# Attention by heads through HBM and a feed-forward stage after it, rewritten as units of 384 tokens with both interleaved on chip

## The chip, the cores and the metric

The kernel runs on one core of one Trainium2 chip. The metric is the device time of one execution in microseconds. Five engines work from queues of their own and wait for one another by semaphores: PE (TensorE, matrix products into PSUM, with weight loads shown as PEld), DVE (VectorE), ACT (ScalarE), POOL (GpSimd) and SP (SyncE, here the queue that issues DMAs).

## What is computed

Attention with a routing mask, then a gated feed-forward over the heads joined together. Batch 4, 8 heads, 768 positions, head size 64, 16 clusters; 3072 tokens of width 512, and 1536 hidden units.

```python
q_assign = argmax(q_n . c_n)            # nearest of 16 centroids, per head
k_assign = argmax(k_n . c_n)
mask = q_assign[:, :, :, None] == k_assign[:, :, None, :]
scores = where(mask, scale * q @ k.T, -1e9)
attn = softmax(scores);  x = attn @ v   # heads side by side: 3072 x 512
xn = x / rms(x) * rms_g
g = xn @ w_gate;  val = xn @ w_val
out = (g * sigmoid(g) * val) @ w_out
```

The norm of q and of k changes no argmax, so neither kernel divides by it.

## The kernel before

There are three stages, one after another. The attention loop (L59 to L138) goes over 4 batches and 8 heads. A head's q, k and v come in as six tiles of 128 positions. PE turns each q and k tile (L93, L97, float32, 64 columns out of 128 positions); ACT makes a bf16 copy and DVE a float32 copy. The cluster scores are float32 products of 16 rows (L108), two for q and two for k; POOL finds the largest of the 16 with an all-reduce over partitions (L113), and DVE makes the one-hot tiles `q_ohT` and `k_ohT` (L114). Then, for each of 6 key tiles and 2 query halves of 384, PE computes the scores (L121, 64 rows) and the mask as a product of one-hots (L123, 16 rows); ACT takes the exponential (L126) and DVE multiplies it with the mask from PSUM into `pT` (L127). The value products (L132) have a column of ones, which gives the softmax sum; DVE divides (L134, L136), and the bf16 result goes to `x_scratch` in HBM.

After the last head the feed-forward weights are loaded and cast (L146 to L161). Then 6 chunks of 512 tokens follow (L169 to L208): `x_sb` is read back, DVE and ACT compute the root mean square, PE transposes (L186), and for each of 12 slices of 128 hidden units four products give `gps` (L194) and four `vps` (L196); ACT computes Silu (L199), DVE the product (L200); 12 products for each 128 tokens give the output (L205), which DVE copies (L207).

The order of instructions within an engine's queue is chosen by the tile scheduler by its own costs; pools of 2 or 3 buffers limit how far the stages overlap. The activation tables change between square root, exponential and Silu (57 loads in the first stage, 44 in the last).

Of the kernel before, what the change touches and what calls it, by code (L numbers as in the profile page):

```python
# [9 lines left out]
F32 = mybir.dt.float32  # L11
F32R = mybir.dt.float32r
BF16 = mybir.dt.bfloat16
AX = mybir.AxisListType.X
ALU = mybir.AluOpType
ACT = mybir.ActivationFunctionType


@with_exitstack
def kernel(  # L20
# [15 lines left out]
    d_model = moe_w_gate.shape[0]  # L36
    d_ff = moe_w_gate.shape[1]
    n_tokens = B * S
    assert H * D == d_model
    P = 128  # L40
    ST = S // P
    scale = 1.0 / (D ** 0.5)
    MM = 384
    NM = S // MM

    x_scratch = nc.dram_tensor("x_scratch", (n_tokens, d_model), BF16, kind="Internal").ap()

    const_pool = ctx.enter_context(tc.tile_pool(name="const", bufs=1))
    ident = const_pool.tile([P, P], BF16)
    make_identity(nc, ident)  # L50
    ident_f32 = const_pool.tile([P, P], F32)
    make_identity(nc, ident_f32)

    with tc.tile_pool(name="attn_sbuf", bufs=2) as sb, \
         tc.tile_pool(name="attn_sbuf1", bufs=2) as sb1, \
         tc.tile_pool(name="attn_psum_a", bufs=2, space=bass.MemoryType.PSUM) as psa, \
         tc.tile_pool(name="attn_psum", bufs=2, space=bass.MemoryType.PSUM) as ps:

        for b in range(B):  # L59
            for h in range(H):  # L60
                q_in = sb.tile([P, ST, D], F32, tag="q_in")
                k_in = sb.tile([P, ST, D], F32, tag="k_in")
                v_in = sb.tile([P, ST, D + 1], F32, tag="v_in")
                nc.sync.dma_start(out=q_in, in_=q[b, h].rearrange("(t p) d -> p t d", p=P))
                nc.sync.dma_start(out=k_in, in_=k[b, h].rearrange("(t p) d -> p t d", p=P))
                nc.sync.dma_start(out=v_in[:, :, :D], in_=v[b, h].rearrange("(t p) d -> p t d", p=P))
                nc.vector.memset(v_in[:, :, D:D + 1], 1.0)
                v_bf = sb.tile([P, ST, D + 1], BF16, tag="v_bf")
                nc.vector.tensor_copy(v_bf, v_in)

                c_in = sb.tile([NC, D], F32, tag="c_in")
                nc.sync.dma_start(out=c_in, in_=centroids[h])
                c_sq = sb.tile([NC, D], F32, tag="c_sq")
                nc.vector.tensor_mul(c_sq, c_in, c_in)
                c_ss = sb.tile([NC, 1], F32, tag="c_ss")
                nc.vector.reduce_sum(c_ss, c_sq, axis=AX)
                c_inv = sb.tile([NC, 1], F32, tag="c_inv")
                nc.vector.reciprocal(c_inv, c_ss)
                nc.scalar.activation(c_inv, c_inv, ACT.Sqrt)
                c_n = sb.tile([NC, D], F32, tag="c_n")  # L80
                nc.vector.tensor_scalar_mul(c_n, c_in, c_inv)
                cnt_ps = psa.tile([D, NC], F32, tag="tmp")
                nc.tensor.transpose(cnt_ps, c_n, ident_f32[:NC, :NC])
                c_nT = sb.tile([D, NC], F32, tag="c_nT")
                nc.vector.tensor_copy(c_nT, cnt_ps)

                qT = sb.tile([D, ST, P], BF16, tag="qT")
                kT = sb.tile([D, ST, P], BF16, tag="kT")
                qT32 = sb.tile([D, S], F32, tag="qT32")
                kT32 = sb.tile([D, S], F32, tag="kT32")  # L90
                for t in range(ST):
                    ttmp = psa.tile([D, P], F32, tag="tmp")
                    nc.tensor.transpose(ttmp, q_in[:, t, :], ident_f32)  # L93
                    nc.scalar.copy(qT[:, t, :], ttmp)  # L94
                    nc.vector.tensor_copy(qT32[:, t * P:(t + 1) * P], ttmp)  # L95
                    ttmp2 = psa.tile([D, P], F32, tag="tmp")
                    nc.tensor.transpose(ttmp2, k_in[:, t, :], ident_f32)  # L97
                    nc.scalar.copy(kT[:, t, :], ttmp2)  # L98
                    nc.vector.tensor_copy(kT32[:, t * P:(t + 1) * P], ttmp2)  # L99

                q_ohT = sb.tile([NC, S], BF16, tag="q_ohT")
                k_ohT = sb.tile([NC, S], BF16, tag="k_ohT")
                qT_flat = qT[:, :, :].rearrange("d t p -> d (t p)")
                for (src_T, ohT) in ((qT32, q_ohT), (kT32, k_ohT)):
                    scT_sb = sb1.tile([NC, S], F32, tag="scT_sb")
                    for m in range(NM):
                        scT_ps = ps.tile([NC, MM], F32, tag="scores")
                        nc.tensor.matmul(scT_ps, lhsT=c_nT,  # L108
                                         rhs=src_T[:, m * MM:(m + 1) * MM],
                                         start=True, stop=True)  # L110
                        nc.scalar.copy(scT_sb[:, m * MM:(m + 1) * MM], scT_ps)  # L111
# [127 lines left out]
```

## Time and profile before

| | |
|---|---|
| median of 3 runs | 1066.64 us (1065.25 to 1066.80) |
| span of the profiled execution | 1065.2 us |
| one head in the steady part of attention | 24.28 us |
| attention, to the last product | about 786 us |
| weights loaded and cast | about 50 us |
| feed-forward | 229.2 us |
| POOL in its all-reduce | 166.1 us, idle before it 598.7 us |
| the chain that ended last, by engine | PE 57%, issue 23%, POOL 7%, DVE 4%, ACT 4%, DMA 4% |

The span runs from the first to the last instruction of one profiled execution; the medians are of runs timed as a whole. In the slices each digit is the busy share of a fortieth of the span in tenths, and PEclk is the clock granted to PE in tenths of full speed, as far as its records go. Busy times of PE are modelled, and overlap: the distance from one start to the next says more than the duration.

### The profile page before, as it was taken

The page shows a single profiled execution, that of the slowest core. Times are in us where ns is not written, and L with a number is a line of the kernel's source. Part 1 is how long each engine was busy: PE and PEld are TensorE (multiplying, and loading weights), DVE is VectorE, ACT ScalarE, POOL GpSimd, SP SyncE. Part 2 cuts the span into 40 slices and gives each one's busy share as a digit, 9 for nine tenths or more (in the row PEclk, how much of TensorE's full clock was granted, in tenths as well). Part 3 has the DMA queues.
Part 4 walks back from the last instruction along what each step waited for, and adds up shares of the span by engine and source line. Part 5 has one row for each costly group of instructions (what it writes and reads, how often), then busy time and mean ns, then how long its engine had stood idle before and what let it go on. Part 6 is the DMA issues. An engine that isn't in the chain of part 4 may idle for free.

```text
span 1065.2 us, 11986 instructions
## 1 busy us (share of the span) xinstructions
PE 908.9 (85%) x3552; PEld 311.0 (29%) x3552; DVE 598.0 (56%) x1665; ACT 508.9 (48%) x1221; POOL 167.2 (16%) x72
## 2 busy tenths in 40 slices
PE   4999999988888999999888898989950599999998
PEld 1222223222222222232222222223210244444443
DVE  3556666566656666666666666655542445534533
ACT  3555555555565544545554455444420456536721
POOL 2112111222211111111222111122200000000000
PEclk9999999995555555555555656555555699999999
DMA  3111111111111111111111111111015310110111
GB/s 75 27 26 27 27 26 27 39 41 29 36 27 35 27 27 27 27 27 34 35 28 35 28 27 27 26 26 21 5 58 210 110 55 11 59 50 30 41 40 40
DMA packets 114098, 41.82 MB, mean 39 GB/s; under 512 B 105328, under 2 KB 108400, under 8 KB 114032
## 3 DMA queue, kind: packets, MB, share of 16 engines
q1 hardware_dynamic: 114032, 41.05, 14.9%
q8 instruction: 28, 0.46, 0.2%
q14 instruction: 38, 0.31, 0.1%
HBM read 31.59 MB, written 9.44 MB: 39 GB/s over the span
## 4 chain that ended last, share of the span: by engine, by line
PE 57%; issue 23%; POOL 7%; DVE 4%; ACT 4%; DMA 4%; POOLq 0%; SPq 0%; DVEq 0%; ACTq 0%
PE scT_ps L108 11%; PE mk_ps L123 9%; PE sc_ps L121 8%; POOL sc_max L113 6%; PE gps L194 6%; PE ops L205 6%; PE vps L196 6%; PE ttmp L97 4%; PE ttmp L93 3%; PE acc L132 3%; DMA wo_tmp<-in_moe_w_out_dram 1%; ACT scT_sb L111 1%; PE tps L186 1%; ACT xnT L187 1%; DMA wtmp<-in_moe_w_val_dram 1%
## 5 line engine op out<-in xcount | busy, mean ns | idle before, releaser
L127 DVE TENSOR_TENSOR pT<-p_e,mk_ps 128x384 bf16<-128x384 bf16 x384 | 209.9, 553 | 157.1 <-PE mk_ps L123 140.3
L113 POOL PARTITION_ALL_REDUCE sc_max<-scT_sb x64 | 166.1, 2602 | 598.7 <-ACT scT_sb L111 597.5
L123 PE MATMUL mk_ps<-q_ohT,k_ohT 16*128 16x384 bf16 x384 | 184.8, 498 | 45.5 <-DVE o_sb L136 41.1
L121 PE MATMUL sc_ps<-qT,kT 64*128 64x384 bf16 x384 | 182.8, 492 | 23.5 <-ACT p_e L126 22.0
L126 ACT ACTIVATE p_e<-sc_ps 128x384 bf16<-128x384 f32 x384 | 168.3, 483 | 18.0 <-DVE pT L127 11.7
L98 ACT CAST kT<-ttmp 64x128 bf16<-64x128 f32 x192 | 49.6, 258 | 175.9 <-PE ttmp L97 174.4
L111 ACT COPY scT_sb<-scT_ps 16x384 f32<-16x384 f32 x128 | 59.6, 466 | 107.9 <-PE scT_ps L108 107.8
L194 PE MATMUL gps<-xnT,wg 128*128 128x512 bf16 x288 | 106.3, 396 | 0.8 <-ACT sg L199 0.2
L196 PE MATMUL vps<-xnT,wv 128*128 128x512 bf16 x288 | 105.9, 394 | 0.0
L132 PE MATMUL acc<-v_bf,pT 128*128 128x65 bf16 x1152 | 93.9, 244 | 7.2 <-DVE o_sb L136 6.6
L123 PEld LDWEIGHTS <-k_ohT 16*128 16x128 bf16 x384 | 37.6, 100 | 212.7 <-issue 138.7
L132 PEld LDWEIGHTS <-pT 128*128 128x128 bf16 x1152 | 77.0, 131 | 57.5 <-DVE qT L95 22.1
L108 PE MATMUL scT_ps<-qT,c_nT 64*16 64x384 f32 x128 | 93.0, 829 | 0.1
L94 ACT CAST qT<-ttmp 64x128 bf16<-64x128 f32 x192 | 49.4, 257 | 86.1 <-PE ttmp L93 85.9
L97 PE MATMUL ttmp<-ident_f,k_in 128*64 128x128 f32 x192 | 79.7, 415 | 9.7 <-DVE kT L99 5.5
L108 PE MATMUL scT_ps<-kT,c_nT 64*16 64x384 f32 x128 | 87.0, 794 | 0.0
L200 DVE TENSOR_TENSOR gvT<-sg,vps 128x512 bf16<-128x512 f32 x72 | 47.7, 685 | 67.8 <-ACT sg L199 67.1
L93 PE MATMUL ttmp<-ident_f,q_in 128*64 128x128 f32 x192 | 79.9, 416 | 1.0 <-DVE qT L95 1.0
L187 ACT COPY xnT<-tps 128x128 bf16<-128x128 bf16 x96 | 21.5, 266 | 105.0 <-DVE wo L161 51.4
L121 PEld LDWEIGHTS <-kT 64*128 64x128 bf16 x384 | 35.9, 101 | 108.1 <-issue 104.8
L186 PE MATMUL tps<-ident,xn 128*128 128x128 bf16 x96 | 19.6, 238 | 55.2 <-ACT xnT L187 53.7
L205 PE MATMUL ops<-wo,gvT 128*128 128x512 bf16 x288 | 66.7, 379 | 0.0
(47 smaller groups left out, 762.1 us busy)
## 6 DMA issues: line engine op xcount, KB each, us to landing
q_in<-in_q_dram SPq DMA_DIRECT2D x32, 192.0 KB, 2.5
k_in<-in_k_dram SPq DMA_DIRECT2D x32, 192.0 KB, 2.5
v_in<-in_v_dram SPq DMA_DIRECT2D x32, 192.0 KB, 2.5
out_dram<-out_sb SPq DMA_DIRECT2D x24, 256.0 KB, 2.0
x_scratch<-o_sb SPq DMA_DIRECT2D x192, 16.0 KB, 1.5
x_sb<-x_scratch SPq DMA_DIRECT2D x24, 128.0 KB, 2.0
wtmp<-in_moe_w_gate_dram SPq DMA_DIRECT2D x1, 3072.0 KB, 10.0
wtmp<-in_moe_w_val_dram SPq DMA_DIRECT2D x1, 3072.0 KB, 10.3
```

The costliest lines, as they stand in the source:

```text
L93: nc.tensor.transpose(ttmp, q_in[:, t, :], ident_f32)
L97: nc.tensor.transpose(ttmp2, k_in[:, t, :], ident_f32)
L108: nc.tensor.matmul(scT_ps, lhsT=c_nT, rhs=src_T[:, m * MM:(m + 1) * MM], start=True, stop=True)
L113: nc.gpsimd.partition_all_reduce(sc_max, scT_sb, NC, bass_isa.ReduceOp.max)
L121: nc.tensor.matmul(sc_ps, lhsT=kT[:, kc, :], rhs=qT_flat[:, m * MM:(m + 1) * MM], start=True, stop=True)
L123: nc.tensor.matmul(mk_ps, lhsT=k_ohT[:, kc * P:(kc + 1) * P], rhs=q_ohT[:, m * MM:(m + 1) * MM], start=True, stop=True)
L126: nc.scalar.activation(p_e, sc_ps, ACT.Exp, scale=scale)
L127: nc.vector.tensor_mul(pT[:, kc, m * MM:(m + 1) * MM], p_e, mk_ps)
L132: nc.tensor.matmul(acc, lhsT=pT[:, kc, qg * P:(qg + 1) * P], rhs=v_bf[:, kc, :], start=(kc == 0), stop=(kc == ST - 1))
L194: nc.tensor.matmul(gps, lhsT=wg[:, dc, fc * P:(fc + 1) * P], rhs=xnT[:, dc, :], start=(dc == 0), stop=(dc == DC - 1))
L196: nc.tensor.matmul(vps, lhsT=wv[:, dc, fc * P:(fc + 1) * P], rhs=xnT[:, dc, :], start=(dc == 0), stop=(dc == DC - 1))
L205: nc.tensor.matmul(ops, lhsT=gvT[:, fc, s * P:(s + 1) * P], rhs=wo[:, fc, :], start=(fc == 0), stop=(fc == FC - 1))
```

## The change

The whole body is rewritten, with an order written out by hand in place of the scheduler's.

The work is cut into units of 384 queries: two units for each batch, eight units in all, and groups of four heads, two for each batch. A *group's preparation* (`group_work`) turns q and k of a head together (`trans`: six float32 transposes a head with 128 columns out, ACT copies them to `qkT`, POOL casts q into `qext` and v into `vbf`, DVE casts k divided by 2048 into `kext`) and computes the cluster scores of four heads as float32 products whose 32 output rows lie in four column strips of the array (`scores_c`). DVE transposes these in blocks of 32, finds the maximum, compares, and transposes back; DMAs put the one-hots under q and k in `qext` and `kext`, as rows 64 to 79, with a row of -1 and +1 below them. So the score product contracts 81 rows: the scaled score, plus 1 where the clusters agree, minus 1. With the exponential's scale of 2048/8 a pair of different clusters gives exp(-256 + score), which is 0, and the mask products and the multiplication by the mask are gone. One exponential covers two key tiles (768 columns in two PSUM banks).

A unit's loop goes over 8 heads with three pairs of key tiles each. Behind each pair stands a part of the list `fill`: the output products of the unit two before, then the feed-forward of the unit before, with the preparation of the group two ahead spread between its pieces. Transposes, clusters, gate, value and output products all use one PSUM pool of three buffers (`ps_g`, tag `gen`). Attention's result stays on chip (`xs`). The root is taken with an integer guess and three Newton steps on DVE; the square sums are taken by ACT. Silu is g/2 (1 + tanh(g/2)), with tanh on ACT and two DVE products, so that the table of the exponential stays; only the last unit uses Silu. The weights are cast by 11 DMAs on POOL's queue, between the first and the second group's preparation.

```diff
+    stage = pool("stage", NSTG)
+    qk32 = pool("qk32", 1)
+    ps_s = pool("ps_s", 2, space=PSUM)
+    ps_a = pool("ps_a", 1, space=PSUM)
+    ps_g = pool("ps_g", 3, space=PSUM)
...
+    def trans(g, h, part):
...
+        for i in range(HT):
+            nc.tensor.transpose(ps[:, i * P:(i + 1) * P], qk[:, t].rearrange("p a d -> p (a d)"), ident_f)
+        nc.scalar.copy(qkT[g][:, h, part * UQ:(part + 1) * UQ], ps)
+        if part:
+            nc.gpsimd.tensor_copy(qext[g % 4][:D, h], qkT[g][:D, h])
+            nc.vector.tensor_scalar_mul(kext[g % 4][:D, h], qkT[g][D:, h], 1.0 / ZS)
+            nc.gpsimd.tensor_copy(vbf[g % 4][:, h, :, :D], vs)
+            load(g * HG + h + NSTG)
...
-                        nc.tensor.matmul(scT_ps, lhsT=c_nT,
-                    nc.gpsimd.partition_all_reduce(sc_max, scT_sb, NC, bass_isa.ReduceOp.max)
+        for h in range(HG):
+            nc.tensor.matmul(ps[32 * h:32 * h + 32], lhsT=cblk[:, h0 + h], rhs=qkT[g][:, h, m * UQ:(m + 1) * UQ],
+        nc.vector.transpose(scT[g][:, m * UQ:(m + 1) * UQ], ps)
+        if m:
+            nc.vector.tensor_reduce(mx, cl, axis=AX, op=ALU.max)
+            nc.vector.tensor_tensor(ohT.rearrange("p (n c) -> p n c", c=NC), cl,
+            nc.vector.transpose(oh, ohT)
+            for h in range(HG):
+                nc.sync.dma_start(out=qext[g % 4][D:D + NC, h], in_=oh[32 * h:32 * h + NC])
...
-                        nc.tensor.matmul(mk_ps, lhsT=k_ohT[:, kc * P:(kc + 1) * P], rhs=q_ohT[:, m * MM:(m + 1) * MM],
-                        nc.vector.tensor_mul(pT[:, kc, m * MM:(m + 1) * MM], p_e, mk_ps)
+            nc.tensor.matmul(ps[:, j, :UQ], lhsT=kext[g % 4][:KR, hh, kc * P:(kc + 1) * P],
+                             rhs=qext[g % 4][:KR, hh, hf * UQ:(hf + 1) * UQ], start=True, stop=True)
+        nc.scalar.activation(pT[u, h][:, 2 * i:2 * i + 2], ps[:, :, :UQ], ACT.Exp, scale=scale * ZS)
...
+    def gv(u, f, val):
...
+        ps = ps_g.tile([P, UQ], F32, tag="gen", name="val" if val else "gate")
+        for c in range(CC):
+            nc.tensor.matmul(ps, lhsT=w[:, c, f * P:(f + 1) * P], rhs=xnT[u][:, c], start=c == 0, stop=c == CC - 1)
...
+                nc.scalar.activation(th, ps, ACT.Tanh, scale=0.5)
+                nc.vector.scalar_tensor_tensor(gu, th, 1.0, ps, op0=ALU.add, op1=ALU.mult)
...
+            nc.vector.scalar_tensor_tensor(gvT[u][:, f], gates[u], 0.5, ps, op0=ALU.mult, op1=ALU.mult)
...
+    for _, f in group_work(0):
+        f()
+    load_weights()
+    for _, f in group_work(1)[:2 * HG]:
+        f()
...
+        for h in range(H):
+            for i in range(3):
+                scores(u, h, i)
+                if i == 0 and (u, h) != (0, 0):
+                    pv(u, h - 1) if h else pv(u - 1, H - 1)
+                    if h == 0:
+                        rms(u - 1)
+                while n < len(fill) and done <= total * (3 * h + i + 1) / gaps:
+                    done += fill[n][0]
+                    fill[n][1]()
+                    n += 1
...
+    pv(NU - 1, H - 1)
+    rms(NU - 1)
+    for _, f in out_work(NU - 2) + ffn_work(NU - 1) + out_work(NU - 1):
```

On PE, in the middle of a head's score loop, before (score, mask and a transpose for the next head by turns):

```order
L121 LDWEIGHTS kT
L121 MATMUL sc_ps<-qT,kT 128x384
L123 LDWEIGHTS k_ohT
L123 MATMUL mk_ps<-q_ohT,k_ohT 128x384
L93 MATMUL ttmp<-ident_f_63,q_in 64x128
L121 LDWEIGHTS kT
```

and in a full unit of the change, from the end of its feed-forward part to the start of the next unit (`val` is a value-branch product, `s` a score, `sc` the clusters of group 4 and `acc` a value product of attention):

```order
L275 LDWEIGHTS wv
L275 MATMUL val<-xnT,wv 128x384
L205 LDWEIGHTS kext_148
L205 MATMUL s<-qext_144,kext_148 128x384
L205 LDWEIGHTS kext_148
L205 MATMUL s<-qext_144,kext_148 128x384
L177 MATMUL sc<-qkT,cblk 32x384 x4
L205 LDWEIGHTS kext_145
L205 MATMUL s<-qext_141,kext_145 128x384
```

The scores no longer take turns with a product of 16 rows; between them stand products of the feed-forward and of the preparation. On ACT, in the score loop of a head before:

```order
L126 ACTIVATE p_e<-sc_ps 128x384 x2
L94 CAST qT<-ttmp 64x128
L126 ACTIVATE p_e<-sc_ps 128x384 x2
L98 CAST kT<-ttmp_1148 64x128
L126 ACTIVATE p_e<-sc_ps 128x384 x2
```

and in a full unit of the change, from the queue's row 112:

```order
L161 COPY qkT<-tq 128x384
L283 ACTIVATE th<-gate 128x384
L207 ACTIVATE pT<-s 128x768
L161 COPY qkT<-tq 128x384
L207 ACTIVATE pT<-s 128x768
L283 ACTIVATE th<-gate 128x384
```

The tanh of a gate stands in line with the exponentials and the copies of the transposes. On POOL the all-reduces of L113 were the whole queue; now the casts of group 0, the weights and the casts of group 1 stand there in this order (the end of group 0 and the start of group 1):

```order
L165 CAST vbf_161<-vs 128x6x64
L145 DMA wg<-in_moe_w_gate_dram 128x1536
L146 DMA wv<-in_moe_w_val_dram 128x1536
...
L148 DMA wo<-in_moe_w_out_dram 128x4x512 x3
L163 CAST qext_142<-qkT 64x768
L165 CAST vbf_162<-vs 128x6x64
```

The second group's casts are now behind 11 DMA issues.

More of the change, by code (lines that the diff above doesn't have):

```diff
@@ new lines @@
+    c_in = const.tile([P, D], F32)
+    nc.sync.dma_start(out=c_in, in_=centroids.rearrange("h c d -> (h c) d"))
+    for n in range(NSTG):
+        load(n)
+    gcol = const.tile([P, CC], F32)
+    nc.sync.dma_start(out=gcol, in_=moe_rms_g.rearrange("(c p) -> p c", p=P), allow_slow_non_contiguous=True)
+    ones = const.tile([P, P], F32)
+    nc.vector.memset(ones, 1.0)
+    cnt = const.tile([P, 32], F32)
+    nc.vector.tensor_tensor_scan(cnt, ones[:, 0:32], ones[:, 0:32], 0.0, op0=ALU.mult, op1=ALU.add)
@@ new lines, with out_mm @@
+    outs = {}
+    def out_mm(u, t, part):
+        b, hf = divmod(u, 2)
+        if part == 0:
+            outs[u] = ps_g.tile([P, DM], F32, tag="gen", name="o")
+        for f in range(4 * part, 4 * part + 4):
+            nc.tensor.matmul(outs[u], lhsT=gvT[u][:, f, t * P:(t + 1) * P], rhs=wo[:, f], start=f == 0, stop=f == FC - 1)
+        if part == 2:
+            o = outp.tile([P, DM], F32, tag="o_sb", name="o_sb")
+            nc.vector.tensor_copy(o, outs[u])
+            rows = out[b * S:(b + 1) * S].rearrange("(p t) f -> p t f", t=ST)
+            nc.sync.dma_start(out=rows[:, hf * HT + t], in_=o)
```

376 lines of the change are left out of this document (221 added, 155 removed).

## Prediction

> **What bounds the kernel now.** I read the busy line, the slices, then windows of one head and of the last stage, and then single products on TensorE (PE).
>
> ```profile
> PE 908.9 (85%) x3552; PEld 311.0 (29%) x3552; DVE 598.0 (56%) x1665; ACT 508.9 (48%) x1221; POOL 167.2 (16%) x72
> PEclk9999999995555555555555656555555699999999
> ```
>
> ```profile
> 137.98:162.25 24.27, 21.84 (x82) 6.82 (x83) 15.14 (x45) 12.23 (x32) 5.15 (x2) 1.00 0.14 29
> 431.64:455.92 24.28, 21.85 (x83) 6.83 (x83) 15.14 (x45) 12.36 (x32) 5.15 (x2) 0.50 0.14 29
> 786.00:836.00 50.00, 2.44 (x28) 1.64 (x27) 13.31 (x20) 0.00 (x0) 0.00 (x0) 0.50 0.52 191
> 836.00:1065.20 229.20, 216.22 (x958) 94.77 (x957) 102.34 (x199) 118.94 (x229) 0.00 (x0) 0.95 0.11 40
> ```
>
> A window's columns are length, then busy time of PE, PEld, DVE, ACT and POOL, and the granted clock. PE is busy 90% of every head (21.85 of 24.28 us); 50 us between the stages go to loading weights; PE is busy 94% of the feed-forward. So PE sets the end, and the question is at which clock. The two heads take the same time although one reads 1.00 and the other 0.50. The single products settle which is right.
>
> ```profile
> 434.73 0.42 PE L97 MATMUL ttmp<-ident_f,k_in 128*64 128x128 f32 x1
> 435.08 1.46 PE L108 MATMUL scT_ps<-kT,c_nT 64*16 64x384 f32 x2
> 436.47 0.84 PE L132 MATMUL acc<-v_bf,pT 128*128 128x65 bf16 x12
> 437.25 0.82 PE L121 MATMUL sc_ps<-qT,kT 64*128 64x384 bf16 x2
> ...
> 446.61 0.50 PE L121 MATMUL sc_ps<-qT,kT 64*128 64x384 bf16 x1
> 447.04 0.50 PE L123 MATMUL mk_ps<-q_ohT,k_ohT 16*128 16x384 bf16 x1
> 447.47 0.50 PE L121 MATMUL sc_ps<-qT,kT 64*128 64x384 bf16 x1
> ```
>
> At half clock: a float32 transpose takes 0.35 us to the next start, a float32 product (two instructions) 1.39, a value product (0.84-0.24)/11 = 0.055, a score behind a score 0.82-0.50 = 0.32, and score and mask by turns 0.43 each.
>
> ```profile
> 529.89 0.81 PE L108 MATMUL scT_ps<-kT,c_nT 64*16 64x384 f32 x2
> 530.63 0.20 PE L83 MATMUL cnt_ps<-ident_f,c_n 16*64 16x16 f32 x1
> ...
> 531.09 0.30 PE L97 MATMUL ttmp<-ident_f,k_in 128*64 128x128 f32 x1
> 531.32 0.82 PE L108 MATMUL scT_ps<-kT,c_nT 64*16 64x384 f32 x2
> 532.44 0.56 PE L132 MATMUL acc<-v_bf,pT 128*128 128x65 bf16 x12 [0.30 <-DVE o_sb L136]
> 532.93 0.49 PE L121 MATMUL sc_ps<-qT,kT 64*128 64x384 bf16 x2
> ```
>
> In a short stretch at full clock the same work takes 0.23, 0.74, (0.56-0.20)/11 = 0.033 and 0.49-0.32 = 0.17. The head at 138 us has the 24.27 us of half clock, so its 1.00 is a missing record: nearly all of attention ran at half clock, busy or not.
>
> ```profile
> 842.01 0.63 PE L196 MATMUL vps<-xnT,wv 128*128 128x512 bf16 x1
> 842.44 0.63 PE L194 MATMUL gps<-xnT,wg 128*128 128x512 bf16 x1
> ...
> 844.01 0.38 PE L194 MATMUL gps<-xnT,wg 128*128 128x512 bf16 x1
> 844.23 0.38 PE L196 MATMUL vps<-xnT,wv 128*128 128x512 bf16 x1
> ```
>
> The feed-forward begins at 0.43 us for 512 columns and goes to 0.215 after three microseconds of dense full-array products: 384 columns are then 0.32 and 0.162.
>
> ```profile
> 522.97:526.39 3.42, 3.42 (x8) 0.69 (x8) 1.63 (x5) 1.41 (x4) 0.00 (x0) 0.50 0.00 0
> 526.42:529.82 3.40, 3.40 (x30) 2.11 (x29) 2.73 (x14) 2.17 (x6) 0.00 (x0) 0.50 0.26 58
> 529.86:536.65 6.79, 3.78 (x24) 1.27 (x22) 5.34 (x10) 4.36 (x11) 5.13 (x2) 1.00 0.19 40
> ...
> 874.60:877.90 3.30, 2.08 (x14) 0.99 (x12) 1.40 (x3) 2.49 (x12) 0.00 (x0) 1.00 0.35 119
> 878.05:881.30 3.25, 3.12 (x11) 1.28 (x10) 1.93 (x3) 1.01 (x4) 0.00 (x0) 0.50 0.11 38
> ```
>
> A stretch busy throughout (523 to 526) with scores, masks and small float32 work does not raise the clock; the next, with 24 of its 30 products of the value kind on all 128 rows and columns, does. A stretch of bf16 transposes with gaps (875 to 878) loses it. I read this as: the clock follows how much of the array is used, not whether PE is busy.
>
> The Trainium skill, page TensorE: Matmul & The Clock Gate, Part 1, has the clock go to full after about 3.4 us of a busy PE; these rows disagree, since a PE busy 90% stayed at half. By the page alone unit 0 below would run at full clock, 16 us sooner.
>
> **The change, part by part.** Nothing of the old order remains, so I rebuild the time from the instructions of the new one: start, unit 0, units 1 to 7, tail.
>
> *PE in a full unit* (2 to 5), at full clock: 48 scores on 81 rows x 0.17 = 8.2 us (the mask products are gone, so no change of shape by turns; if weight loads show after all, 0.43-0.32 = 0.11 more each, 5.3); 144 value products x 0.033 = 4.8; 96 gate and value-branch products x 0.162 = 15.5; 36 output products x 0.215 = 7.8; 12 bf16 transposes of 128 columns at 0.1 at most (a quarter of the 0.43 for 512) = 1.2; 24 float32 transposes with 128 stationary columns in place of 64, between 0.23 and 0.35, taken as 0.30, 7.2 in all; 8 column-tiled float32 products. These last are not in the trace: all four abreast they cost 2 x 0.74 = 1.5, one after another 5.9. The two instructions of a product share a tile, so in order only neighbours of different tiles overlap, five instruction times of eight: 3.7. Sum 48.4. Unit 1 has no output products: 40.6. Units 6 and 7 prepare no group: 37.5 each. Seven units: 40.6 + 4 x 48.4 + 75.0 = 309.
>
> The Trainium skill, page TensorEngine Tiling (Array Packing), Key Properties, lets tiles load and multiply in parallel but drains PE when the tiling mode changes. With four abreast the sum below would lose some 23 us, with only drains it would gain about that; no row here shows either.
>
> *ACT and DVE in a full unit.*
>
> ```profile
> L127 DVE TENSOR_TENSOR pT<-p_e,mk_ps 128x384 bf16<-128x384 bf16 x384 | 209.9, 553 | 157.1 <-PE mk_ps L123 140.3
> L126 ACT ACTIVATE p_e<-sc_ps 128x384 bf16<-128x384 f32 x384 | 168.3, 483 | 18.0 <-DVE pT L127 11.7
> L111 ACT COPY scT_sb<-scT_ps 16x384 f32<-16x384 f32 x128 | 59.6, 466 | 107.9 <-PE scT_ps L108 107.8
> L199 ACT ACTIVATE sg<-gps 128x512 f32<-128x512 f32 x72 | 40.8, 596 | 41.9 <-PE gps L194 41.7
> L200 DVE TENSOR_TENSOR gvT<-sg,vps 128x512 bf16<-128x512 f32 x72 | 47.7, 685 | 67.8 <-ACT sg L199 67.1
> ...
> 437.44 1.38 DVE L69 CAST v_bf<-v_in 128x390 bf16<-128x390 f32 x1
> ...
> masks.py:199 POOL TENSOR_SCALAR_AFFINE_SELECT ident_f<-ident_f 128x128 f32<-128x128 f32 x1 | 0.3, 282 | 0.0
> ```
>
> An exponential of 768 is 0.76 (0.48 plus 0.32 for 384 more elements, less overlap): ACT has 24 x 0.76 + 8 x 0.47 + 12 x 0.48 + 3 x 0.6 = 29.6 us. DVE has 24 gate products x 0.55 = 13.2, cluster work of about 4 (reduce, compare and its three 32x32 transposes, which the trace lacks; I price them as the 0.55 and 0.69 of a pass over PSUM, and twice that would add 3), casts to kext 4 x 0.5, and some 10 in copies, normalisation and the small steps of the root: 29. Both hide behind 48 us of PE. A DVE cast beside POOL stretches to 1.38 (last row but one); four of these a unit are hidden too. POOL's 8 casts are bounded by 0.28 us per 128 columns (its rows for the identity) times six, 10 us a unit, hidden. The SP queue issues some 20 DMAs a unit, under 10 us.
>
> *The new wait.* Gate, value, transposes, clusters and outputs all take turns in three PSUM buffers. A gate's buffer is held from its product's end through a tanh (after 0 to 0.8 us behind an exponential) and a DVE product (0.55, behind up to one other): about 1.9 us. PE uses one such buffer each 0.95 us in this part of a unit, so a gate must be free after 1.9: no slack. Queued behind the waiting product are the next scores, and ACT's exponentials wait for those. I charge 0.4 us for each of 12 gates, 10% of a unit: 31 us over seven. Bounds: 0, and a hold of twice that (1.9 x 12 = 23 us a unit). In unit 1 no output products cover the root's chain (squares, 12 small steps, three scalings): 6 us more.
>
> *Start, unit 0, tail.*
>
> ```profile
> q1 hardware_dynamic: 114032, 41.05, 14.9%
> 5.41 0.37 DVE L69 CAST v_bf<-v_in 128x390 bf16<-128x390 f32 x1 [4.52 <-DMA v_in<-in_v_dram]
> 3.43 0.54 SPq L65 DMA_DIRECT2D k_in<-in_k_dram  x1
> out_dram<-out_sb SPq DMA_DIRECT2D x24, 256.0 KB, 2.0
> wtmp<-in_moe_w_gate_dram SPq DMA_DIRECT2D x1, 3072.0 KB, 10.0
> ```
>
> 41 MB in 14.9% of the span is 259 KB per us, 2.3 us for a head. 24 transposes at half clock with the wider load (0.35 + 0.14) are 11.8 us, so with the first data at 5 us, group 0 is turned by 17; its cluster products take 7 (24); group 1's transposes another 12, over the one-hot chain and its DMAs: 36. Unit 0 has 48 x 0.32 + 126 x 0.055 + 24 x 0.49 + two groups' clusters 14 = 48 us of PE at half clock, 26 at full clock (then ACT binds too). It lacks dense products; I take 42, nearer the half clock. POOL's 11 weight DMAs stand ahead of group 1's casts: at SP's 0.54 us each they are done long before head 4 needs them at 57; if POOL waits for all 9.4 MB at the last row's 300 KB per us, 31 us, the loss is 4. I take 0. The tail: output of unit 6 7.8 over the root's chain, transposes 1.5, 24 x 0.65 + 1 = 16.6, output 7.8, copy 0.7, DMA 2, hand-overs 1.6: 38.
>
> Sum: 36 + 42 + 309 + 31 + 6 + 38 = 462, and 1.4 for what lies between the span of 1065.2 and the median of 1066.64: **463 us**. The profiled execution stands that close to the median, so nothing is scaled.
>
> **Rivals.** *Clock stays at half* (0.08): the 90% busy attention speaks for it, the rise within 3 us of dense gate products against. A full unit is then 48 x 0.32 + 144 x 0.055 + 96 x 0.32 + 36 x 0.43 + 24 x 0.49 + 7 + 1.3 = 89 us, unit 1 74, units 6 and 7 70.6: 571, with start 36, unit 0 48 and a tail of 66: 722. The same page of the Trainium skill, under its second failure mode, has PE fall back between bursts when PSUM buffers cycle; by it the time would lie between this and the forecast.
>
> *The ring binds* (0.14): a hold of 3.8 us costs 23 us in each of seven units: 463 + 7 x 23 - 31 = 593. For it: ACT and DVE are 60% busy and in order, each gate crosses both.
>
> *The columns don't tile* (0.15): the products run one after another: 2.2 us in five units, 4 at the start, 8 in unit 0: 486.
>
> *Nothing stalls* (0.06): no ring loss, tiles four abreast, unit 0 at full clock: 463 - 31 - 23 - 10 = about 400.
>
> *Slower* (0.01): the ring works as one buffer at half clock, so PE, ACT and DVE of a unit add up: 89 + 30 + 29 = 148 for four, 126, and 2 x 123 is 964, plus 36 + 70 + 78: 1148. It decides only if each product waits for the release of the one before; 3 buffers and full clock each alone prevent it.
>
> **How the numbers follow.** Forecast 0.55, the rest 0.01. The range goes from nothing stalls (400) to the ring with serial columns (593 + 23): 400 to 615, leaving out the half clock. This measurement tells 0.2% from no change; all cases but one are hundreds of microseconds faster: faster 0.98, same 0.005, slower 0.015.
>
> **What would show it.** PE busy about 90% of units 1 to 7 at a granted clock near 1.00, gate products 0.16 apart, units of 53 us; waits of PE for a gate's DVE product of about 5 us a unit; four cluster products within 1.9 us; first exponential at 36 us. Gate products 0.32 apart, or PE waits over 15 us a unit, would prove it wrong.

## Result and the profile after

| | before | after |
|---|---|---|
| median | 1066.72 us (4 runs, 1065.25 to 1067.49) | 422.09 us (4 runs, 420.24 to 424.04) |
| ratio to before | | 0.396, 95% interval 0.394 to 0.398 |
| span of the profiled execution | 1065.2 us | 422.2 us |

The forecast was 463 us, and the range 400 to 615. The time lies inside it, 41 us under the forecast. How well that sum was made is a question of its terms, because some of them missed in opposite directions. Times and ratios here and below leave out executions in a slower state; only the profile of the run with the mask apart is of one (596 us, mean clock 0.87).

First the busy line and the slices of the changed kernel, from its page:

```profile
PE 354.2 (84%) x2995; PEld 213.8 (51%) x3009; DVE 232.4 (55%) x509; ACT 237.7 (56%) x404; POOL 59.6 (14%) x85
PE   3701188579997999799988999799979999999896
PEclk9965559869998999999999999999999999999899
DMA  7999985604222233014312220200011001000101
```

TensorE (PE) is busy for 354 us in place of 909, ScalarE (ACT) for 238 in place of 509, VectorE (DVE) for 232 in place of 598. The first five slices (10.6 us each) show something else than the rest: PE at 1 or less in three of them, the DMA engines at 9 in four. Then PE is busy for most of each slice, mostly at full clock.

Next the windows by stage: start, units 0 to 7, tail. A unit runs from its first score to the next unit's. Columns as in the prediction: length, busy time of PE, PEld, DVE, ACT and POOL, granted clock, DMA share, GB/s.

```profile
0.00:53.10 53.10, 13.96 (x65) 8.93 (x65) 11.90 (x30) 10.13 (x19) 21.12 (x37) 0.73 1.03 204
53.20:79.80 26.60, 23.76 (x230) 12.85 (x231) 11.18 (x19) 20.48 (x32) 6.66 (x8) 0.84 0.77 183
79.84:122.80 42.96, 36.50 (x340) 23.72 (x340) 25.40 (x58) 29.64 (x51) 6.62 (x8) 0.88 0.27 64
122.80:168.98 46.18, 43.28 (x379) 26.39 (x377) 30.17 (x63) 29.21 (x51) 6.06 (x8) 0.96 0.28 74
...
215.13:259.60 44.47, 41.95 (x378) 25.74 (x376) 29.75 (x64) 29.11 (x51) 6.39 (x8) 1.00 0.18 50
...
380.00:422.20 42.20, 35.78 (x202) 18.76 (x202) 17.16 (x42) 10.52 (x21) 0.00 (x0) 0.96 0.10 38
```

Beside the forecast's terms (its ring loss of 31 spread evenly over seven units, 4.4 each):

| stage | forecast | measured | difference |
|---|---|---|---|
| start | 36 | 53.2 | +17 |
| unit 0 | 42 | 26.6 | -15 |
| unit 1 (with the root's chain) | 51 | 43.0 | -8 |
| units 2 to 5 | 211 | 181.3 | -30 |
| units 6 and 7 | 84 | 75.9 | -8 |
| tail | 38 | 42.2 | +4 |

The differences are -61 us and +21 us: that the time came within 41 us of the forecast is in part luck.

PE's own waits, summed over the span:

```profile
PE tq L160 <- DMA qk<-in_k_dram: 30.8, 6, 22.1
PE s L205 <- issue: 7.5, 5, 2.3
PE tx L264 <- DVE xn L255: 6.0, 1, 6.0
PE s L205 <- ACT pT L207: 4.9, 3, 2.2
```

Columns are total, count and longest. No gate or value product waits for a PSUM buffer in the list: the ring loss is absent, but for 0.4 us of a transpose in unit 2 and 2.0 us in the tail (below). The waits of a score for "issue" and for an exponential were not forecast. Five of these eight, 2.2 us each, are one and the same wait, early in each of units 2 to 6:

```profile
222.58 0.48 PE L205 MATMUL s<-qext,kext 81*128 81x384 bf16 x2 [2.25 <-issue]
```

```profile
127.22 0.63 ACT L237 ACTIVATE junk<-x 128x512 bf16<-128x512 f32 x1 [3.01 <-DVE x L227]
...
129.36 1.49 ACT L207 ACTIVATE pT<-s 128x768 bf16<-128x768 f32 x2
```

The first fence is the timeline of PE in unit 4, the second that of ACT at the start of unit 2, where PE waits 2.25 us as well. `rms` places three squares in ACT's queue behind the first exponential of a unit. They wait 3.0 us until DVE has written the last heads into `x`, and the exponentials behind them wait too, although their scores are ready. PE then has no score buffer to write.

The gate part of unit 4, timeline of PE, DVE and ACT in order of time:

```profile
236.07 0.81 PE L275 MATMUL gate<-xnT,wg 128*128 128x384 bf16 x4
...
236.72 0.49 PE L160 MATMUL tq<-ident_f,qk 128*128 128x128 f32 x3
236.97 0.48 ACT L283 ACTIVATE th<-gate 128x384 f32<-128x384 f32 x1
237.08 0.81 PE L275 MATMUL val<-xnT,wv 128*128 128x384 bf16 x4
...
237.49 0.55 DVE L285 SCALAR_TENSOR_TENSOR gu<-th,gate 128x384 f32<-128x384 f32 x1 [0.47 <-ACT th L283]
237.72 0.49 PE L205 MATMUL s<-qext,kext 81*128 81x384 bf16 x2
238.05 0.81 PE L275 MATMUL gate<-xnT,wg 128*128 128x384 bf16 x4
```

Four gate products take 0.65 us to the next start, 0.162 each. Three float32 transposes take 0.36, 0.12 each. The gate's product ends near 236.72, DVE has read it at 238.04: a hold of 1.32 us. The next gate, the fourth user of the ring, starts at 238.05, straight behind two scores that fill the time. There was no slack indeed, but no loss.

### The profile page after: what moved, and what is told of

Its sections match the earlier page's. It is cut to its first block, busy times and chain, and to the rows that moved or that the text cites. A ratio compares the mean times of both kernels' runs of the same rounds, so it can differ in the third digit from the quotient of the medians.

```text
span 422.2 us, 7646 instructions
## 1 busy us (share of the span) xinstructions
PE 354.2 (84%) x2995; PEld 213.8 (51%) x3009; DVE 232.4 (55%) x509; ACT 237.7 (56%) x404; POOL 59.6 (14%) x85
## 4 chain that ended last, share of the span: by engine, by line
PE 69%; DMA 9%; DVE 7%; ACT 6%; SPq 4%; issue 3%; POOL 0%; DVEq 0%; ACTq 0%
PE gate L275 15%; PE val L275 14%; PE s L205 13%; PE o L299 11%; PE acc L221 8%; DMA qk<-in_k_dram 6%; PE tq L160 4%; ACT pT L207 3%; ACT junk L237 2%; PE sc L177 2%; SPq L80 1%; PE tx L264 1%; DVE o_sb L302 1%; DMA vs<-in_v_dram 1%; SPq L81 1%
## 5 line engine op out<-in xcount | busy, mean ns | idle before, releaser
L207 ACT ACTIVATE pT<-s 128x768 bf16<-128x768 f32 x192 | 153.7, 811 | 63.0 <-PE s L205 61.8
L205 PE MATMUL s<-qext,kext 81*128 81x384 bf16 x384 | 96.1, 334 | 17.0 <-issue 7.5
L275 PE MATMUL gate<-xnT,wg 128*128 128x384 bf16 x384 | 80.4, 330 | 0.0
L275 PE MATMUL val<-xnT,wv 128*128 128x384 bf16 x384 | 79.1, 328 | 0.0
L285 DVE SCALAR_TENSOR_TENSOR gu<-th,gate 128x384 f32<-128x384 f32 x84 | 46.5, 553 | 54.0 <-ACT th L283 53.5
L299 PE MATMUL o<-wo,gvT 128*128 128x512 bf16 x274 | 70.5, 388 | 0.8
L221 PE MATMUL acc<-vbf,pT 128*128 128x65 bf16 x1152 | 50.6, 195 | 2.0 <-ACT pT L207 1.5
L283 ACT ACTIVATE th<-gate 128x384 f32<-128x384 f32 x84 | 41.1, 489 | 19.9 <-PE gate L275 19.9
L290 DVE SCALAR_TENSOR_TENSOR gvT<-gu,val 128x384 bf16<-128x384 f32 x84 | 46.5, 554 | 9.5 <-PE val L275 3.1
L275 PEld LDWEIGHTS <-wv 128*128 128x128 bf16 x384 | 36.7, 98 | 23.1 <-issue 1.4
L164 DVE TENSOR_SCALAR kext<-qkT 64x768 bf16<-64x768 f32 x32 | 23.2, 729 | 43.3 <-ACT qkT L161 42.2
```

Source lines behind the costliest of these rows:

```text
L205: nc.tensor.matmul(ps[:, j, :UQ], lhsT=kext[g % 4][:KR, hh, kc * P:(kc + 1) * P], rhs=qext[g % 4][:KR, hh, hf * UQ:(hf + 1) * UQ], start=T ...
L207: nc.scalar.activation(pT[u, h][:, 2 * i:2 * i + 2], ps[:, :, :UQ], ACT.Exp, scale=scale * ZS)
L221: nc.tensor.matmul(acc[:, h % 2, t], lhsT=pT[u, h][:, kc, t * P:(t + 1) * P], rhs=vbf[g % 4][:, hh, kc], start=kc == 0, stop=kc == ST - 1)
L275: nc.tensor.matmul(ps, lhsT=w[:, c, f * P:(f + 1) * P], rhs=xnT[u][:, c], start=c == 0, stop=c == CC - 1)
L283: nc.scalar.activation(th, ps, ACT.Tanh, scale=0.5)
L285: nc.vector.scalar_tensor_tensor(gu, th, 1.0, ps, op0=ALU.add, op1=ALU.mult)
```

## Experiments

Where one time is given it is the median. All ratios are to the kernel before on the same chip.

**The start: weights later.** The weights' DMAs are issued between the preparations of groups 0 and 1; is the start late because of them?

```diff
-    load_weights()
     for _, f in group_work(1)[:2 * HG]:
         f()
+    load_weights()
```

> The 11 weight DMAs on POOL's queue stand behind the preparation of group 1 instead of ahead of it. Theory (the first score at 53.2 us, 17 later than predicted, is late because the loads of heads 6 and 7 share the DMA engines with 9.4 MB of weights): the loads of these heads land some 15 us sooner, the first score comes at 33 to 40 us, and the time falls by 10 to 18 us, to 404 to 412, less whatever unit 1 then waits for weights. Rival (the loads are late by their place in SP's queue alone, behind 18 loads and 8 row copies at 0.6 us each): the first score moves by under 3 us and the time stays within 1% of 422.

Measured: 421 and 422 us, ratio 0.396 (0.395 to 0.397). No gain, where 10 to 18 us were expected. The first score did move, from 53.2 to 33.3, so the weights were what held it up; but unit 0 lasted 48.2 us in place of 26.6:

```profile
33.31:81.50 48.19, 27.34 (x231) 15.29 (x232) 11.21 (x19) 21.05 (x32) 11.82 (x17) 0.66 1.02 202
```

```profile
PE tq L160 <- DMA qk<-in_k_dram: 19.3, 7, 8.1
PE s L205 <- DMA kext<-oh: 14.8, 2, 11.2
```

PE is busy for 27 of 48 us, while the DMA engines are full at 202 GB/s. The two longest of these waits, 8.1 us for a head of group 2 and 11.2 us for the one-hots of group 1, lie in unit 0: the wait went there from the start, as unit 0 also prepares group 2.

**The ring of three buffers.** One edit, `ps_g` with 2 buffers in place of 3.

> The PSUM pool of gates, values, transposes, clusters and outputs has two buffers in place of three. The trace shows no wait inside the gate part of a unit, where a gate's buffer comes round again 1.3 us after its last product. Theory (a gate is held about 1.2 us, so three buffers hide it just and two, which come round after 0.4 to 0.7 us, do not): 0.5 to 0.8 us for each of 24 gate and value products of seven units, 40 to 100 us more. Rival (the hold is much shorter than the predicted 1.9 us and two buffers do as well): under 2% more. Rival (three buffers already bind): over 120 us more.

Measured: 457.5 us, ratio 0.430 (0.429 to 0.431); 35 us more, a little under the 40 to 100 expected. A full unit goes from 44.5 to 51.3 us, and the ring's waits appear among PE's:

```profile
PE val L275 <- ACT qkT L161: 5.7, 12, 0.6
...
PE gate L275 <- DVE gu L285: 3.5, 18, 0.2
```

So the ring works as a resource as the prediction had it, and it takes the third buffer away to make it bind. With three it costs next to nothing.

**The column strips.** The cluster products of four heads are made 128 columns wide, with zeros for the other heads, and accumulate, one after another on the whole array.

```diff
...
-            nc.tensor.matmul(ps[32 * h:32 * h + 32], lhsT=cblk[:, h0 + h], rhs=qkT[g][:, h, m * UQ:(m + 1) * UQ],
-                             start=True, stop=True)
+            nc.tensor.matmul(ps, lhsT=cblk[:, h0 + h].rearrange("p a c -> p (a c)"), rhs=qkT[g][:, h, m * UQ:(m + 1) * UQ],
+                             start=h == 0, stop=h == HG - 1)
```

> The four cluster products of a half are no longer put into four column strips: each has 128 columns of weights, with zeros outside its own strip, and the four accumulate in one PSUM tile. The result is the same, and nothing else moves. Theory (the strips work abreast, four products in the time of one, so the prediction's five of eight was too dear): a group's eight products take 8 x 0.74 = 5.9 us in place of 1.6 at full clock, so 4.3 us more in each of five units and 8 in unit 0, with the start hidden behind DMAs: about 450 us. Rival (the strips save nothing, the product is fast for another reason): the time stays within 1%.

Measured: 442 to 447 us, ratio 0.421 (0.418 to 0.423), a little under the 450 expected. Unit 4 takes 47.9 us in place of 44.5. The timeline of PE shows the price itself, first the changed kernel, then this one:

```profile
213.93 0.49 PE L205 MATMUL s<-qext,kext 81*128 81x384 bf16 x2
214.35 0.85 PE L177 MATMUL sc<-qkT,cblk 128*32 128x384 f32 x8
215.13 0.50 PE L205 MATMUL s<-qext,kext 81*128 81x384 bf16 x2
```

```profile
268.93 2.74 PE L178 MATMUL sc<-qkT,cblk 128*128 128x384 f32 x8
271.51 0.49 PE L206 MATMUL s<-qext,kext 81*128 81x384 bf16 x2
```

Four float32 products (eight instructions) take 0.78 us to the next start in strips and 2.58 without: 0.32 for each instruction in a row, and the time of about two and a half such instructions in strips. Strips run four abreast, with a little left over. The Trainium skill, TensorEngine Tiling (Array Packing), Key Properties, says both that tiles load and multiply in parallel and that a change of mode drains PE. The trace agrees with the first. Of the second it shows only small prices: the two scores ahead of the strips take 0.42 us to the next start where two in the gate part above take 0.33, so the change into strips costs some 0.1 us, and 0.78 less two instructions (0.65) leaves at most 0.13 for the change back.

**The squares behind the third exponential** (from unit 2 on; unit 1 as before).

```diff
-                    if h == 0:
-                        rms(u - 1)
+                if h == 0 and u and i == (0 if u == 1 else 2):
+                    rms(u - 1)
```

> From unit 2 on, the square sums of the unit before are issued on ACT behind the third exponential of the unit in place of the first. Theory (the one wait of PE in a unit, 2.25 us at its start, is the exponentials standing behind the squares, which wait for DVE's normalisation): the wait goes in six units, 10 to 14 us less, about 410. Rival (the squares only move, and the transposes of the normalised rows then wait for the root's chain): within 1% of 422.

Measured: 410.8 us, ratio 0.386 (0.385 to 0.387), 11 us less than the changed kernel. The wait at a unit's start is gone, and with it the stretches of half clock that followed it:

```profile
210.40:252.40 42.00, 41.61 (x378) 25.76 (x376) 29.54 (x64) 29.18 (x51) 6.39 (x8) 1.00 0.19 53
```

A full unit (4 here) is now 41.6 us of PE in 42.0, so to make it shorter takes less work on PE. Units 2 and 3 last 43.5 and 43.0: there a transpose waits 1.3 us until DVE has copied an output out of the ring.

**Silu everywhere.** `last = True` in `gv`: all units take ACT's Silu and one DVE product, as the kernel before did, and no tanh.

> The gate's activation is Silu in all units, as it was before the change in every unit, so ScalarE alternates Exp and Silu inside each of units 1 to 6. Theory: each change of function costs ScalarE a table load beside the work; with 12 gates a unit spread between the exponentials some 24 changes a unit at 1 to 1.3 us add 24 to 31 us to the 29.7 us that ScalarE is busy in a unit of 46, so ScalarE becomes the bound at 54 to 61 us a unit: 480 to 560 us in all. The rival: the change of table is hidden or cheap, and since VectorE loses 12 instructions of 0.55 us a unit the time stays within 2% of the 422 us of the changed kernel.

Measured: 597.7 us, ratio 0.562 (0.560 to 0.563), 176 more, over the estimate of 480 to 560. Groups of the page and a window of unit 4:

```profile
L280 ACT ACT_TABLE_LOAD x85 | 109.1, 1283 | 2.9 <-PE gate L275 1.5
L207 ACT ACT_TABLE_LOAD x85 | 109.1, 1283 | 1.5
```

```profile
286.52:355.07 68.55, 49.96 (x381) 28.43 (x377) 22.23 (x51) 60.76 (x75) 6.39 (x8) 0.90 0.12 32
```

A table load takes 1.28 us, and there are 170 in these two groups, 24 of them in unit 4: 218 us of ACT in all. ACT is busy for 61 us of a unit, as estimated; but the unit is 69 us, because ACT at 89% is now waited for by PE and waits for it in turn, and PE loses clock (0.90). Of the parts of the change undone alone this is the dearest.

**The mask as a product of its own.** The 81 rows of a score are split into 64 rows of keys and 17 rows of one-hots, two products that accumulate.

```diff
-            nc.tensor.matmul(ps[:, j, :UQ], lhsT=kext[g % 4][:KR, hh, kc * P:(kc + 1) * P],
-                             rhs=qext[g % 4][:KR, hh, hf * UQ:(hf + 1) * UQ], start=True, stop=True)
+            for r in (slice(0, D), slice(D, KR)):
+                nc.tensor.matmul(ps[:, j, :UQ], lhsT=kext[g % 4][r, hh, kc * P:(kc + 1) * P],
+                                 rhs=qext[g % 4][r, hh, hf * UQ:(hf + 1) * UQ], start=r.start == 0, stop=r.start > 0)
```

> Same mask, but not inside one contraction: the 64 rows of keys and the 17 rows of one-hots are two products that accumulate in the same place, so 48 more score products a unit. Theory that a product's time goes by the 384 columns that stream through it and not by its rows: +48 x 0.162 = 7.8 us a unit, 8 units, +62 us, so about 485 us. The rival, that a product of 17 rows is nearly free beside the one of 64 rows (it uses other rows of the array): within 10 us of 422. A dearer outcome, up to 104 more (526 us), if the second half also drains the array each time.

Measured: 578 to 581 us, ratio 0.545 (0.543 to 0.547); about 158 more, beyond even the dearer outcome. Two causes show, in two windows of unit 0 and that of unit 3, and on PE's timeline:

```profile
50.00:80.00 30.00, 26.92 (x123) 9.18 (x123) 5.36 (x8) 10.08 (x14) 2.63 (x4) 0.50 0.52 123
80.00:110.00 30.00, 30.00 (x147) 11.16 (x147) 6.16 (x11) 12.05 (x17) 4.99 (x6) 0.50 0.24 60
...
256.92:317.79 60.87, 60.87 (x428) 28.49 (x425) 30.20 (x63) 30.37 (x51) 6.40 (x8) 1.00 0.21 56
```

```profile
269.95 1.13 PE L206 MATMUL s<-qext,kext 64*128 64x384 bf16 x4
271.00 1.04 PE L300 MATMUL o<-wo,gvT 128*128 128x512 bf16 x4
```

At full clock four products by turns of 64 and 17 rows take 1.05 us, 0.26 each in place of 0.162, and the unit goes to 60.9. The weight loads show where the 0.10 goes, first the changed kernel, then this one:

```profile
213.77 0.26 PEld L205 LDWEIGHTS <-kext 81*128 81x128 bf16 x2
```

```profile
270.21 0.09 PEld L206 LDWEIGHTS <-kext 17*128 17x128 bf16 x1 [0.17 <-issue]
```

In the changed kernel the load starts 0.16 us ahead of its product (213.93, above) and so lies beside the product before; here it starts with its product, 0.26 after 269.95, and its 0.09 us come on top. Why it is not taken early is not shown; a mere change in the number of rows is not enough for it, as the scores on 81 rows take 0.162 beside gate products on 128. And the clock stays at half through two stretches in which PE is busy for 26.9 and 30.0 of 30 us. In the runs that the time is from, a mean clock of 0.90 over some 579 us is still about 116 us at half clock.

**Every score twice.** The same number of products as in the run above, all over 81 rows; the second overwrites the first.

```diff
-            nc.tensor.matmul(ps[:, j, :UQ], lhsT=kext[g % 4][:KR, hh, kc * P:(kc + 1) * P],
-                             rhs=qext[g % 4][:KR, hh, hf * UQ:(hf + 1) * UQ], start=True, stop=True)
+            for _ in range(2):
+                nc.tensor.matmul(ps[:, j, :UQ], lhsT=kext[g % 4][:KR, hh, kc * P:(kc + 1) * P],
+                                 rhs=qext[g % 4][:KR, hh, hf * UQ:(hf + 1) * UQ], start=True, stop=True)
```

> Every score product is issued twice over all 81 rows (the second overwrites the first), so the count of score products is that of the run with 64 and 17 rows apart, and the rows of the array stay the same from product to product. If the price of the split mask is the count alone, this costs as much: about 580 us, and 0.26 us for each score product. If the price is in the change of rows between neighbours, each product stays at 0.162 us: 48 x 0.162 = 7.8 us a unit, 8 units, 484 us (475 to 490), at full clock, since the array is used more and not less.

Measured: 471.4 us, ratio 0.443 (0.442 to 0.444); 49 more, a little under the 475 to 490 expected. Two windows, of unit 0 from 62.3 on and of unit 4:

```profile
62.30:85.00 22.70, 22.04 (x232) 14.31 (x229) 11.12 (x19) 17.84 (x28) 6.66 (x8) 1.00 0.63 148
...
237.19:287.70 50.51, 49.23 (x428) 30.44 (x424) 30.00 (x63) 30.02 (x51) 6.39 (x8) 1.00 0.16 44
```

Its full unit is 50.5 us: 6.0 more, where 48 products of 0.162 are 7.8; part of the difference is the wait at the unit's start, 1.3 us here in place of 2.25. So a second product as such costs 49 us of the 158. That products on 64 and on 17 rows stand by turns costs 0.10 us more for each of 96, 10 us a unit (60.9 against 50.5), an estimated 83 us in eight. What is left, 26 us, fits the clock: about 116 us at half clock there and 54 here (mean clock 0.943 over 471 us) is a loss of some 31. In the profiles, unit 0 stays at half clock to its end there and goes to full here, after 8.7 us, with the same number of products.

**Attention and feed-forward apart.** Attention of four units, then their feed-forward and output, twice. One staging buffer fewer, four buffers of `xn`; else the same instructions.

```diff
-        if u >= 2:
-            fill += out_work(u - 2)
...
-        fill += spread(ffn_work(u - 1), prep) if u >= 1 else prep
+        fill += prep
...
+        if u % 4 == 3:
+            pv(u, H - 1)
+            rms(u)
+            for w in range(u - 3, u + 1):
+                for _, f in ffn_work(w) + out_work(w):
+                    f()
```

> Attention of four units, then the four feed-forwards and output products, and the same again: the same instructions, with attention and feed-forward not interleaved. One part of the theory: in the attention of a unit alone ScalarE's 24 exponentials of 0.81 us are 19.5 us while TensorE has 7.9 + 4.7 us of products (and about 5 us of transposes and clusters), so TensorE waits 2 to 7 us of each unit that the interleave fills: +16 to +56 us. Other part: the use of the array in attention alone (scores 81 rows of 128 for 7.9 of 20 us, values 65 columns of 128 for 4.7 of 20 us, about 0.33) falls under the use after which the full clock is granted, so attention stretches fall to half clock and each product doubles there: the attention of a unit 25 us in place of 20, another +40 us. Both: 480 to 520 us, with granted clock near 0.6 in the attention stretches. Clock by busy time alone: full clock throughout, 440 to 475 us. No effect of the interleave: 422 us.

Measured: 497.8 us, ratio 0.467 (0.466 to 0.469), 76 more, in the range for both parts. How they share it was not isolated; by the mean clocks, 0.855 against 0.933, some 144 us at half clock against 56, at most an estimated 44 of the 76 us are clock. Windows of the attention of unit 1, of a part of the first feed-forward, and of the attention of units 4, 6 and 7:

```profile
81.01:108.87 27.86, 21.82 (x233) 14.62 (x233) 14.19 (x34) 23.32 (x39) 6.27 (x8) 0.88 0.38 94
...
215.00:240.00 25.00, 24.55 (x144) 13.39 (x142) 16.33 (x32) 5.59 (x12) 0.00 (x0) 1.00 0.09 32
...
273.63:296.45 22.82, 18.57 (x215) 11.77 (x214) 8.66 (x16) 20.34 (x32) 6.39 (x8) 1.00 0.36 91
324.31:353.01 28.70, 23.32 (x193) 13.36 (x194) 6.67 (x24) 20.57 (x31) 0.00 (x0) 0.59 0.03 8
353.01:381.14 28.13, 24.02 (x192) 14.63 (x192) 6.25 (x23) 19.85 (x30) 0.00 (x0) 0.50 0.01 1
```

The feed-forward alone is PE at 98% and full clock, with ACT busy for 5.6 of 25 us. Attention alone is ACT at 70 to 90%. Where attention stands alone with nothing else on PE (units 6 and 7), the clock is at half and the unit takes 28 us although ACT needs 20; where a group's preparation stands between, in unit 4, it kept full clock, and in units 1 and 5 it had 0.88. The expectation of 0.6 in all attention was right for units 6 and 7 alone.

**The order of the start.** From the first experiment: not only the weights, but all that unit 0 does not need goes behind what it needs. The loads of group 2 are issued in unit 0's fill, group 2 is prepared at the start of unit 1 (and so covers the root's chain), the weights go behind group 1's transposes.

```diff
-            load(g * HG + h + NSTG)
+            n = g * HG + h + NSTG
+            if n < 2 * HG or g > 1:
+                load(n)
...
-            prep = group_work(2)
+            prep = [(1.0, lambda n=n: load(n)) for n in range(2 * HG, 2 * HG + NSTG)]
...
+        if u == 1:
+            fill += group_work(2)
```

> Only the order of the start is changed: weights after group 1's transposes, loads of group 2 and later not before unit 0, group 2's transposes and clusters at the start of unit 1 instead of in unit 0. Theory: the first 80 us of the changed kernel are bound by DMA volume in the wrong order (heads that unit 2 needs and weights are ahead of what unit 0 needs), so unit 0 starts at about 33 us, runs without waits in 20 to 24 us, unit 1 starts at 53 to 58 us, its root's chain (6 us) is covered by group 2's transposes, and it ends at 98 to 106 us in place of 122.8: 398 to 408 us in all. The rival, that the volume itself binds up to the end of unit 1: waits for the loads or the weights take the place inside unit 1, its end stays near 118 us, and the time is 415 to 422 us.

Measured: 407.5 us, ratio 0.384 (0.382 to 0.385), 15 less.

```profile
28.56:56.90 28.34, 21.86 (x191) 11.21 (x190) 6.82 (x12) 19.58 (x27) 8.26 (x13) 0.68 0.98 178
56.90:106.54 49.64, 43.75 (x380) 28.38 (x380) 32.74 (x65) 33.58 (x59) 12.94 (x16) 0.85 0.74 172
```

The first score is at 28.6, unit 1 starts at 56.9 and ends at 106.5 in place of 122.8. Unit 0 is longer than the 20 to 24 us expected: it waits 3.9 us for the one-hots of group 1, and with less work between its scores it has a mean clock of 0.68. The wait of 6 us for the root's chain is gone.

**Both.** The last kernel joined with the later squares.

> The start in the order of the run with weights after group 1 and loads of group 2 later, together with the root's squares behind the third exponential from unit 2 on. The first took 422.1 to 407.5, the second to 410.8. If they are about different stretches (the first 107 us; six starts of units behind it), the gains add: 407.5 - 11.3 = 396, range 393 to 400. If the second gain is partly the same wait as the first: 400 to 405.

Measured: 393.0 us (392.6 to 393.7), ratio 0.3695 (0.3688 to 0.3701). The two gains add, as expected (393 to 400); this version beats both kernels. Its windows of units 2 to 7 all show a clock of 1.00, and unit 4 lasts 42.0 us.

## Why the prediction came out as it did

*What bounds it.* Right: PE sets the end from unit 1 on, busy for 94% of unit 4 (41.95 of 44.47), at clock 1.00, with gate products 0.162 apart. The clock rival (722 us) is out.

*The start, 36 us: wrong, 53.2, and the step that failed is that it was a sum of PE's work.* Transposes and clusters were priced on PE, with 2.3 us of transfer for a head beside them and nothing for the weights. On the chip PE waits 22 us for one head of group 1. SP's queue and the chain that ended last show where it is:

```profile
21.88 6.32 SPq L81 DMA_DIRECT2D vs<-in_v_dram  x1
...
31.27 10.68 SPq L81 DMA_DIRECT2D vs<-in_v_dram  x1
...
48.89 0.60 SPq L191 DMA_DIRECT2D qext<-oh  x1
```

```profile
8.24 4.65 DMA qk<-in_k_dram
...
21.01 19.86 DMA qk<-in_k_dram
```

A load issued at 21.0 lands 19.9 us later, where one issued before the weights took some 5, as 4.7 MB of weights go at the same time; SP's next issues block for 6 and 11 us each, and the one-hots of group 0, for which the first score waits, stand behind the loads of four more heads. The prediction bounded the weights at a loss of 4 us, and looked at POOL's casts, not at the loads that share the DMA engines. By volume it could have been seen: eight heads of 0.59 MB and 4.7 MB of weights (the page's software queue) are 9.4 MB, which at the 204 GB/s of the first window is 46 of the 53 us; with the two further heads that stand ahead of the one-hots it is 52. Moving the weights alone moved the wait; ordering all loads by need cut PE's waits for DMAs, from group 1's transposes to the end of unit 1, from 31 to 15 us.

*Unit 0, 42 us: wrong, 26.6.* The forecast chose a value near half clock and had 14 us of cluster products. The clock was at half for the first 8.5 us of the unit and full for the other 18.1, and clusters and transposes cost a good deal less than priced (next point). Start and unit 0 together are 79.8 against 78: two errors that cancelled, by luck.

*PE in a full unit, 48.4: too large, 41.6* (PE's busy time where the wait is gone). Float32 transposes were taken as 0.30 and are 0.12: 24 of them, 4.3 us. Clusters were taken as five of eight instruction times, 3.7 us, and go four abreast, 0.78 for four products and 1.6 for the eight: 2.1 us. Scores (0.162 to 0.167), value products (0.033), gate and output products (0.162, 0.215) were right, and so was the work of ACT (29.6 forecast, 29.1 measured in unit 4) and DVE (29 and 29.8), hidden behind PE.

*The ring, 31 us: wrong in size, 0 for gates and values.* The step that failed is the hold of 1.9 us and 0.4 us charged for each gate; the hold was 1.32, and the scores between two gates covered what was left. That the ring has no slack is borne out: with two buffers the same kernel loses 35 us.

*The wait that was not foreseen.* The prediction listed what is queued behind a waiting gate, but not behind the waiting squares on ACT. They cost 2.2 us in each of units 2 to 6, 11 us in all, and in units 2 and 3 some clock behind them: 0.96 over the 46.2 us of unit 2 is 3.7 us at half. Moving them behind the third exponential gave 11 us.

*The root's chain in unit 1, 6 us:* right, 6.0 in the waits. *The tail, 38:* 42.2, with a mean clock of 0.96. The last root's chain is hidden behind the output of unit 6, as forecast. But then PE waits 2.0 us for a ring buffer: a transpose needs that of unit 6's last output, and DVE's copy of it waits for one of the two `o_sb` buffers, which an output DMA still holds. The first gate products behind this wait stand at half clock.

```profile
391.48 0.69 DVE L302 COPY o_sb<-o 128x512 f32<-128x512 f32 x1 [1.60 <-DMA out_dram<-o_sb]
```

*The rivals.* "Nothing stalls" (400) came nearest in its terms, and the time of 422 lies between it and the forecast: no ring loss, strips abreast, unit 0 short; but the start took 17 us back, and the squares 11. "Columns don't tile" is refuted by 0.78 against 2.58 us, "the ring binds" by the waits.

*The clock.* The reading that the clock follows the use of the array and not PE's busy time stood its test: with the mask apart PE is busy for 30.0 of 30 us and the clock remains at half, and with as many products on 81 rows it goes to full in the same unit. The Trainium skill, TensorE: Matmul & The Clock Gate, Part 1, has about 3.4 us of a busy PE bring full clock; these windows disagree as the rows before did. What share of rows and columns is the threshold was not isolated, nor why a group's preparation held full clock in unit 4 of the run apart.

*The signs named ahead.* PE busy about 90% near full clock, gates 0.16 apart and four clusters within 1.9 us came true; units of 53 us (44.5), waits for a gate's DVE product (none) and a first exponential at 36 us (after 53) did not.

## What to carry to other kernels

Sum the bytes that the first stage needs, and those that merely stand ahead of them in a queue, before summing its engine work: moving one load moved the wait here, ordering by need halved it. Of each instruction that may wait, ask on its own engine what is queued behind it; three squares of 0.63 us cost 2.2 us in each of five units only by their place. Pack what can be packed into one contraction: here 64 and 17 rows by turns in place of 81 cost 158 us, first in products, then in weight loads that no longer lay beside the product before, and last in clock.

## What was not expected of the hardware

- Two accumulating products on 64 and on 17 other rows by turns took 0.26 us each at full clock, where products that all use 81 rows took 0.162; the weight load of 0.09 us started with its product in place of 0.16 us ahead of it.
- Four float32 products in strips of 32 columns took 0.78 us, against 2.58 on the whole width.
- Float32 transposes of 128x128 in groups of three took 0.12 us each at full clock.
- An issue of a load on SP blocked its queue for up to 10.7 us while the DMA engines were full at some 200 GB/s.
- Changing ACT's table cost 1.28 us for each load (170 of them), and the unit with 24 loads was 24 us longer, less than 24 x 1.28 = 31; ACT had been idle for a third of the unit before.
